# A planned attention kernel: its layout table found anew, five transfer charges raised, and a guard on the units that VectorE takes

## The chip, the cores and the metric

The kernel runs on one core of one Trainium2 chip. The core has TensorE (PE, matrix products), VectorE (DVE), ScalarE (ACT), GpSimd (POOL) and SyncE (SP, which here only issues transfers). The metric is the device time of one execution in microseconds (us); lower is better.

## The reference

Two attention layers read the same x of 2048 tokens by 640, each with 32 heads of 20. A is full softmax attention. B lets each token see 8 earlier ones at a distance of 2. A gate per token mixes the two.

```python
g = sigmoid((x * gate_w).sum(-1, keepdims=True))
# A: o = softmax(q @ k.T * 20**-0.5) @ v over all 2048 keys, 32 heads
# B: keys at pos - 2*w, w = 0..7, masked below 0; softmax over these 8
# both: q, k, v = x @ wqkv, and o (heads side by side) @ wo
return g * A(x, A_wqkv, A_wo) + (1 - g) * B(x, B_wqkv, B_wo)
```

Nearly all the work is A: 32 heads of 2048 by 2048 scores, each through an exponential.

## The kernel before

**Groups and units.** A is cut into 32 groups: four stretches of 512 queries (qc) by eight sets of four heads (q). A group has 64 units; a unit is 128 keys by 512 queries of one head. TensorE makes a unit's scores in PSUM (line 1600), its exponential is taken, and the product with the values (with a column of ones for the denominators) is summed in one PSUM bank, `obank` (line 1669).

**Two ways to an exponential.** ScalarE takes two or three units in one instruction, which is called a tile here (line 1624; 1024 or 1536 elements a partition). The other way is VectorE's: a unit that rides in the third bank of a tile's scores becomes a 16-bit integer whose bits are read as bf16 (line 1614, `uD`), and three shifted copies of it (line 863, `eD`) are averaged with it by values that GpSimd has weighted (line 855, `vS`). Four such units, with the same keys, make a quad. A quad is opened in `wanted()` for the present group or the next one, from the last keys of the group backwards; the products take the quads strictly in the order in which they were opened (`pv_slot`).

**What else runs.** Between the tiles come the projections of A (lines 660 to 792), layer B in eight units of 256 tokens (products of q with shifted k on VectorE at line 935, their sums on TensorE at 945, maxima at 970 to 978, exponentials at 983, products with v at 1032, their sums at 1042, the division at 1065), the end of each group (transpose of `obank` at 824, division on GpSimd at 830 and 836, transpose back at 838, transfer to `oTd` at 841), and the products with both wo (`gen_fold`; for the last 512 tokens `gen_prefold` and `gen_prefold2`, whose results the tail completes at line 1148). Where TensorE would stand idle too long the planner puts products that nobody reads (`filler`, line 1690).

**The planner.** No order is written by hand. While the program is built, `task()` keeps a clock for each engine with a charged duration for each instruction, and a loop over tiles picks what comes next. Its choices hang on 18 numbers (how long TensorE may be kept from the next scores, when a third unit or a ride is taken, priorities of the side work, the load below which fillers are put in, and so on). `PLAN` gives them by tile number: an entry holds from its tile on until the next entry. The clock and the choices exist only at build time. The chip runs five fixed lists of instructions, one an engine, each in order, which wait for each other by semaphores alone.

**Lists of transfers.** Five places issue several small transfers in a row from SP, which count as one task: rows of q to `qT` (730), bounds to `qT` (770), a group's output to `oTd` (841), B's reciprocals to `rB` (1018) and their spreading to all partitions (1020). Each is charged 2.0 us and some time per transfer until all have landed.

**The end.** `gen_wl` loads the last rows of A's wo into a buffer (`woA_l`) that is also an output buffer: GpSimd clears it (1114) once the output has left, and SP loads it (1115). `gen_prefold` makes the products of the last 512 tokens in three pieces (columns 0 to 511 of token blocks 0 and 1, then columns 512 to 639 of all four blocks), and `gen_prefold2` blocks 2 and 3. The third piece and `gen_prefold2` need B's last unit.

Of the kernel before, what the change touches and what calls it, by code (L numbers as in the profile page):

```python
# [50 lines left out]
    0: ((0.29, 0.69), 0.16, 1.0, 5.5, 0.94, -1.37, 0.17, 9.99, 5.5, 6.98, 0.6, 0.62, 5.69, 5.04, 0.0, 0.62, 2, -1.5),  # L51
    5: ((0.29, 0.69), 0.01, 1.0, 6.6, 1.12, -1.6, 0.17, 11.8, 2.0, 7.54, 0.6, 0.62, 4.85, 4.42, 0.0, 0.65, 2, -3),
    15: ((0.32, 0.64), 0.16, 1.0, 2.5, 0.94, -1.41, -0.97, 11.8, 7.0, 8.62, 0.62, 0.47, 4.4, 4.29, 0.0, 0.54, 2, -3),
    20: ((0.29, 0.69), 0.16, 1.0, 2.5, 0.94, -1.41, -0.97, 11.8, 7.0, 8.62, 0.62, 0.62, 5.69, 5.04, 0.0, 0.54, 2, -3),
    30: ((0.3, 0.63), 0.25, 1.0, 2.5, 1.39, -1.06, -0.43, 7.4, 7.0, 8.84, 0.7, 0.51, 4.4, 4.81, -0.2, 0.69, 1, -3),
    35: ((0.32, 0.68), 0.31, 2.5, 5.5, 0.76, -1.58, -0.5, 11.8, 7.0, 6.64, 0.35, 0.39, 4.4, 4.35, 0.0, 0.66, 2, -3),
    40: ((0.34, 0.69), 0.01, 1.0, 5.5, 0.94, -1.37, 0.17, 9.99, 7.0, 7.54, 0.6, 0.62, 5.69, 5.04, 0.0, 0.65, 2, -3),
    45: ((0.26, 0.66), 0.39, 1.0, 2.5, 0.49, -1.34, -0.97, 7.4, 7.0, 8.25, 0.52, 0.47, 4.4, 4.0, 0.0, 0.71, 3, 0.0),
    50: ((0.26, 0.75), 0.39, 1.0, 2.5, 0.49, -1.34, -0.97, 7.4, 7.0, 8.25, 0.52, 0.47, 4.4, 4.0, 0.0, 0.71, 3, 0.0),
    60: ((0.26, 0.75), 0.39, 1.0, 2.5, 0.49, -1.34, -0.97, 6.5, 7.0, 8.25, 0.43, 0.47, 4.4, 4.0, 0.0, 0.71, 3, 0),  # L60
    70: ((0.26, 0.75), 0.39, 1.0, 2.5, 0.81, -1.34, -0.97, 6.5, 7.0, 8.25, 0.43, 0.47, 4.4, 4.0, 0.0, 0.71, 0, 0),
    75: ((0.25, 0.75), 0.39, 1.0, 2.5, 0.81, -1.34, -0.97, 6.61, 7.0, 8.25, 0.43, 0.47, 4.4, 4.0, 0.0, 0.71, 0, 0),
    85: ((0.32, 0.64), 0.16, 1.0, 6.6, 0.94, -1.41, -0.97, 11.8, 7.0, 8.62, 0.62, 0.47, 4.4, 4.29, 0.0, 0.54, 3, -3),
    90: ((0.3, 0.63), 0.07, 5.5, 6.3, 0.94, -1.06, 0.05, 7.4, 2.0, 8.96, 0.66, 0.67, 4.79, 5.42, -0.14, 0.53, 1, -1.5),
    100: ((0.3, 0.63), 0.07, 2.5, 6.3, 0.94, -1.06, 0.05, 11.8, 2.0, 6.64, 0.44, 0.67, 3.3, 3.84, -0.14, 0.66, 1, -3),
    105: ((0.3, 0.63), 0.07, 5.5, 6.3, 0.94, -1.06, 0.05, 9.51, 2.0, 8.96, 0.64, 0.67, 3.3, 5.42, -0.14, 0.53, 1, -1.5),
    110: ((0.32, 0.64), 0.16, 5.5, 2.5, 0.94, -1.06, 0.05, 11.8, 2.0, 8.96, 0.62, 0.67, 3.3, 5.42, -0.14, 0.53, 2, -3),
    115: ((0.3, 0.66), 0.25, 2.5, 2.5, 0.73, -1.17, 0.49, 7.4, 2.0, 5.3, 0.63, 0.52, 5.64, 3.24, 0.0, 0.61, 1, 0),
    120: ((0.29, 0.69), 0.16, 1.0, 1.0, 0.94, -1.37, 0.17, 9.99, 7.0, 7.54, 0.6, 0.62, 5.69, 5.04, 0.0, 0.65, 2, -3),
    125: ((0.29, 0.69), 0.16, 1.0, 1.0, 0.94, -1.37, 0.17, 9.99, 7.0, 7.54, 0.6, 0.53, 5.69, 5.04, 0.0, 0.65, 2, 0),  # L70
    135: ((0.29, 0.6), 0.16, 1.0, 1.0, 0.94, -1.37, 0.17, 9.99, 7.0, 7.54, 0.6, 0.47, 5.69, 5.04, 0.0, 0.65, 2, 0),
    140: ((0.29, 0.6), 0.16, 1.0, 1.0, 0.94, -1.37, 0.17, 9.99, 7.0, 7.54, 0.6, 0.47, 5.69, 5.2, 0.0, 0.6, 2, 0),
    145: ((0.29, 0.6), 0.16, 1.0, 1.0, 0.94, -1.37, 0.17, 9.99, 2.0, 8.47, 0.6, 0.47, 5.69, 5.2, 0.0, 0.6, 2, 0),
    150: ((0.23, 0.7), 0.25, 2.5, 2.5, 0.83, -1.37, 0.49, 7.4, 5.5, 6.11, 0.45, 0.67, 7.13, 5.42, 0.0, 0.61, 1, 0),
    155: ((0.23, 0.7), 0.16, 1.0, 2.5, 0.94, -1.37, 0.49, 7.4, 5.5, 7.54, 0.45, 0.67, 5.69, 5.04, 0.0, 0.54, 1, -3),
    180: ((0.23, 0.7), 0.16, 1.0, 2.5, 0.94, -1.37, 0.49, 7.4, 5.5, 7.54, 0.45, 0.67, 5.69, 5.04, 0.0, 0.54, 1, 1),
    185: ((0.23, 0.7), 0.16, 5.5, 2.5, 0.94, -1.37, 0.49, 7.4, 5.5, 7.54, 0.45, 0.67, 5.69, 5.04, 0.0, 0.54, 1, -3),
    190: ((0.23, 0.7), 0.28, 5.5, 1.0, 0.94, -1.6, -0.5, 7.4, 5.5, 7.54, 0.52, 0.67, 4.64, 5.04, 0.0, 0.54, 1, -1.5),
    200: ((0.32, 0.64), 0.35, 5.5, 1.0, 0.94, -1.6, -0.5, 11.8, 7.0, 7.54, 0.52, 0.67, 4.4, 5.04, 0.0, 0.54, 1, -1.5),
    210: ((0.33, 0.64), 0.35, 5.5, 1.0, 1.02, -1.6, -0.5, 11.8, 7.0, 7.54, 0.52, 0.67, 4.4, 5.04, 0.0, 0.54, 1, -1.5),  # L80
    215: ((0.31, 0.76), 0.28, 2.5, 1.0, 0.72, -1.6, -0.65, 9.86, 7.0, 7.05, 0.52, 0.55, 5.68, 3.17, 0.0, 0.64, 2, -6),
    220: ((0.34, 0.68), 0.38, 2.5, 1.0, 0.94, -1.06, 0.05, 7.4, 7.0, 10.69, 0.6, 0.55, 3.3, 5.42, 0.0, 0.61, 1, -1.5),
    225: ((0.34, 0.68), 0.38, 2.5, 1.0, 0.82, -1.06, -0.35, 9.79, 7.0, 10.69, 0.61, 0.44, 4.4, 5.42, 0.0, 0.61, 1, 1),
    245: ((0.34, 0.68), 0.38, 2.5, 1.0, 0.82, -1.06, -0.35, 6.21, 7.0, 10.69, 0.61, 0.44, 4.4, 5.42, 0.0, 0.53, 1, 1),
    250: ((0.44, 0.72), 0.28, 2.5, 1.0, 1.21, -1.6, -0.5, 9.86, 7.0, 6.01, 0.45, 0.54, 6.04, 3.66, 0.0, 0.87, 0, -6),
    255: ((0.34, 0.68), 0.38, 2.5, 1.0, 0.94, -1.06, 0.05, 7.4, 7.0, 10.69, 0.6, 0.55, 3.3, 5.42, 0.0, 0.61, 1, -1.5),
    260: ((0.3, 0.63), 0.39, 1.0, 2.5, 0.94, -1.26, -0.43, 7.8, 7.0, 6.29, 0.7, 0.73, 5.56, 4.87, -0.08, 0.67, 2, -3),
    265: ((0.3, 0.63), 0.16, 1.0, 1.0, 0.94, -1.46, -0.29, 6.5, 5.5, 7.16, 0.43, 0.75, 6.57, 3.11, -0.2, 0.43, 1, 0),
    270: ((0.3, 0.63), 0.25, 1.0, 1.0, 0.94, -1.29, -0.29, 6.5, 5.5, 7.16, 0.43, 0.75, 6.57, 3.83, -0.2, 0.43, 1, 0),
    275: ((0.3, 0.63), 0.25, 1.0, 1.0, 0.94, -1.29, -0.29, 6.5, 5.5, 7.16, 0.43, 0.75, 6.57, 3.83, -0.2, 0.56, 1, 0),  # L90
    280: ((0.3, 0.63), 0.25, 2.5, 1.0, 0.94, -1.29, 0.49, 6.5, 5.5, 7.16, 0.43, 0.75, 5.56, 3.83, 0.0, 0.61, 1, 0),
    285: ((0.3, 0.63), 0.38, 2.5, 1.0, 0.94, -1.29, 0.49, 6.5, 5.5, 7.16, 0.43, 0.63, 5.56, 4.3, 0.0, 0.61, 1, 0),
    290: ((0.23, 0.63), 0.38, 2.5, 1.0, 0.94, -1.29, 0.49, 6.5, 5.5, 7.16, 0.43, 0.63, 5.56, 4.3, 0.0, 0.61, 0, 0),
    295: ((0.23, 0.63), 0.1, 2.5, 1.0, 0.94, -1.29, 0.49, 6.5, 5.5, 7.16, 0.43, 0.63, 5.56, 4.3, 0.0, 0.61, 0, 0),
    300: ((0.23, 0.63), 0.1, 2.5, 1.0, 0.94, -1.29, 0.49, 6.5, 5.5, 7.16, 0.43, 0.63, 5.56, 4.3, 0.0, 0.77, 0, 0),
    305: ((0.23, 0.66), 0.25, 2.5, 2.5, 0.94, -1.05, 0.49, 7.4, 2.0, 5.3, 0.43, 0.43, 5.56, 3.83, -0.1, 0.61, 1, 0),
# [283 lines left out]
def _build(ctx, nc, A_x, A_wqkv, A_wo, B_wqkv, B_wo, gate_w, out):  # L380
# [252 lines left out]
    done = {}  # L633
# [840 lines left out]
    def wanted(js):  # L1474
# [8 lines left out]
        if not dopen:  # L1483
# [4 lines left out]
            for g in range(cur["g"], min(NG, cur["g"] + 2)):  # L1488
                lo, hi = ahead[g]
                t_end += (4 * hi - lo - 4) * UNIT  # L1490
                if done.get(("q", g)) and t_end >= now + DTIME:
                    break
# [370 lines left out]
```

## Time and profile before

| | |
|---|---|
| median of 3 runs | 810.18 us (809.9 to 811.21) |
| the profiled execution's own time | 810.18 us |
| its span (first to last instruction) | 808.3 us |
| ACT busy | 779.0 us |
| PE busy | 749.0 us |
| DVE busy | 721.9 us |
| POOL busy | 129.3 us |
| share of the 16 DMA engines' span taken by the main queue | 17.0% |
| tiles of 1024 and of 1536 | 449 and 258 |
| rides (`uD`) and shifted copies (`eD`) | 376 and 282 |
| filler products on TensorE | 480 (120 sets of four) |
| granted TensorE clock, mean | 0.996 |

Busy time adds up an engine's records. Records of ScalarE and VectorE reach into those that follow, so a busy share near 100% still hides short waits; the distance between two starts shows what one instruction really takes. TensorE's four 32-column products run side by side, so four records cost about what one does. The column "idle before" names what ended an engine's last wait.

### The profile page before, as it was taken

Reading aid. Unit: us, or ns where it says so; the run is one execution under the profiler, and the core shown is the slowest. Engines: PE = TensorE matmul, PEld = TensorE weight load, DVE = VectorE, ACT = ScalarE, POOL = GpSimd, SP = SyncE. Lnnn points to the kernel's source line nnn. Section 1 sums busy time; section 2 is a strip of 40 time slices with the busy share of each in tenths; the row PEclk is TensorE's granted clock in tenths of the full one; section 3 lists DMA queues with packets and bytes.
Section 4 is the critical chain, followed back from the end, with each engine's and each line's share of the span. In section 5 each row is a group of like instructions: output and inputs, shape, how many; then the busy total and the mean of one; then the engine's idle time right before and its main releaser. Section 6 shows DMA issues by size and latency. Waiting matters only on the chain.

```text
span 808.3 us, 28593 instructions
## 1 busy us (share of the span) xinstructions
PE 749.0 (93%) x12063; PEld 285.9 (35%) x12065; DVE 721.9 (89%) x1236; ACT 779.0 (96%) x739; POOL 129.3 (16%) x193
## 2 busy tenths in 40 slices
PE   8999999999899898999999898999899899999987
PEld 5432222333233332333334323432334343234323
DVE  7587996589999999999999999899999999998865
ACT  4999999999999999999999999999999999999994
POOL 6011011011121110212112111121111212111010
PEclk9999999999999999999999999999999999999999
DMA  9112112300013131110013101313010310300221
GB/s 310 45 28 44 43 29 47 76 13 20 5 39 73 34 69 34 21 25 6 22 37 70 24 18 30 77 22 68 7 39 26 71 23 18 74 7 23 51 55 37
DMA packets 61458, 35.50 MB, mean 44 GB/s; under 512 B 27220, under 2 KB 60132, under 8 KB 61332
## 3 DMA queue, kind: packets, MB, share of 16 engines
q1 hardware_dynamic: 61044, 33.36, 17.0%
q8 instruction: 96, 1.57, 0.8%
q10 hardware_dynamic: 288, 0.33, 0.1%
q14 instruction: 30, 0.25, 0.1%
HBM read 12.00 MB, written 2.62 MB: 18 GB/s over the span
## 4 chain that ended last, share of the span: by engine, by line
PE 34%; DVE 32%; ACT 20%; issue 11%; SPq 1%; DMA 1%; POOL 0%; DVEq 0%; ACTq 0%; POOLq 0%
ACT ebuf L1624 20%; DVE uD L1614 12%; PE score L1600 10%; DVE eD L863 9%; PE side L623 9%; PE obank L1669 9%; PE score L623 3%; DVE kvw L935 3%; DVE kvw L1032 2%; DVE qkvB L909 2%; SPq L917 1%; PE obank L1690 1%; PE score L1315 1%; PE obank L523 1%; PE side L1042 1%
## 5 line engine op out<-in xcount | busy, mean ns | idle before, releaser
L1624 ACT ACTIVATE ebuf<-score 128x1024 bf16<-128x1024 f32 (+1 forms) x707 | 767.2, 1233 | 8.6 <-PE score L1600 7.4
L1600 PE MATMUL score<-qT,kT 32*128 32x512 bf16 x2048 | 278.5, 385 | 32.5 <-ACT ebuf L1624 19.5
L1614 DVE TENSOR_SCALAR uD<-score 128x512 int16<-128x512 f32 x376 | 247.3, 677 | 12.3 <-PE score L1600 11.9
L863 DVE TENSOR_SCALAR eD<-uD 128x2048 int16<-128x2048 int16 x282 | 200.2, 731 | 1.7 <-PE obank L1669 0.6
L1669 PE MATMUL obank<-ebuf,vA 128*21 128x512 bf16 x1672 | 155.7, 387 | 4.8 <-DVE oTt L824 1.3
L1600 PEld LDWEIGHTS score<-qT,kT 32*128 32x128 bf16 x2048 | 69.6, 91 | 255.7 <-ACT ebuf L1624 177.7
L855 POOL TENSOR_TENSOR vS<-vA,vw 128x252 bf16<-128x252 bf16 x94 | 70.0, 748 | 317.5 <-PE obank L1669 261.5
L1669 PE MATMUL obank<-eD,vS 128*21 128x512 bf16 x1128 | 99.4, 382 | 0.0
L623 PE MATMUL side<-xT,wBs 128*32 128x256 bf16 x2400 | 96.5, 282 | 2.3 <-DVE qkvB L909 1.5
L623 PEld LDWEIGHTS side<-xT,wBs 128*32 128x32 bf16 x2400 | 68.1, 142 | 33.1 <-issue 16.3
L1669 PEld LDWEIGHTS obank<-ebuf,vA 128*21 128x21 bf16 x1672 | 36.8, 89 | 88.0 <-issue 60.4
L830 POOL TENSOR_TENSOR rcp<-rcp,gA 128x16 f32<-128x16 f32 x31 | 8.3, 268 | 292.2 <-DVE rcp L828 292.2
L935 DVE TENSOR_TENSOR kvw<-qkvB 128x2048 bf16<-128x2048 bf16 x40 | 48.6, 1233 | 0.0
L1032 DVE TENSOR_TENSOR kvw<-kvw,eB 128x2048 bf16<-128x2048 bf16 x40 | 47.9, 1213 | 0.5 <-DMA kvw<-qkvB 0.5
L909 DVE CAST qkvB<-side 128x512 bf16<-128x512 f32 (+1 forms) x72 | 41.6, 587 | 5.1 <-PE side L623 4.9
L1669 PE MATMUL obank<-uD,vA 128*21 128x512 bf16 x376 | 36.8, 382 | 0.1
L1669 PEld LDWEIGHTS obank<-eD,vS 128*21 128x21 bf16 x1128 | 27.9, 92 | 17.1 <-issue 1.0
L836 POOL TENSOR_TENSOR oN<-oTt,rcp 128x512 bf16<-128x512 f32 x31 | 32.7, 1053 | 2.4
L824 DVE STREAM_TRANSPOSE oTt<-obank 128x512 f32<-128x512 f32 x32 | 22.6, 706 | 4.3 <-PE obank L1669 4.3
L623 PE MATMUL side<-woBp,oB 128*32 128x512 bf16 (+1 forms) x500 | 25.4, 304 | 0.9 <-DVE outsb L1193 0.5
L623 PE MATMUL side<-woA_d,oTd 128*32 128x512 bf16 (+1 forms) x496 | 25.5, 303 | 0.0
L623 PE MATMUL side<-xT,kvw 128*32 128x512 bf16 x310 | 24.3, 382 | 0.9 <-DVE qkvB L660 0.3
(180 smaller groups left out, 517.4 us busy)
## 6 DMA issues: line engine op xcount, KB each, us to landing
kvw<-qkvB SPq DMA_DIRECT2D x128, 80.6 KB
WqP<-in_A_wqkv_dram SPq DMA_DIRECT2D x16, 160.0 KB
wBs<-in_B_wqkv_dram SPq DMA_DIRECT2D x1, 2400.0 KB
oTd<-oN SPq DMA_DIRECT2D x108, 20.0 KB
qT<-dst SPq DMA_DIRECT2D x104, 20.0 KB
out_dram<-outsb SPq DMA_DIRECT2D x12, 160.0 KB
kvw<-in_A_wqkv_dram SPq DMA_DIRECT2D x2, 800.0 KB
oTd<-in_A_x_dram SPq DMA_DIRECT2D x2, 640.0 KB
```

The source lines that it names most:

```text
L623: ins = e.matmul(o[j:k, :], l(j) if callable(l) else l[:, j:k], r, start=(first and i == 0), stop=(last and i == n - 1), skip_group_check= ...
L824: T("dve", 0.625, lambda e: e.transpose(oTt[:, :], obank[:, :]), reads=["obank"], writes=["oTt"])
L836: T(en, c2, lambda e: e.tensor_tensor(oo, ii, ib, ALU.mult), reads=["rcp", "oTt"], writes=["oN0"])
L855: T("pool", 0.607, lambda e: e.tensor_tensor(vS[:, d % 2, :, :], _ap(vA, (kb * NQ + q) * 4 * DV, [[0, K - 1], [1, 4 * DV]]), _ap(vw, 0, [[ ...
L863: T("dve", 0.065 + 0.1334 * n, lambda e, k=k, sl=sl: e.tensor_scalar(eD[:, sl % NS, 0:512 * n].bitcast(I16), uD[d % 2][:, 0:512 * n].bitca ...
L909: t = TB(dvc(n * TOK), lambda e, o=o, i=i: e.tensor_copy(o, i), reads=[("side", b)], writes=[key])
L935: TB(dvc(CH, 2), lambda e: e.tensor_tensor(o, i0, i1, ALU.mult), reads=["qB", "kB"], writes=[("prod", i)] + (["WkA", "WvA", ("WkP", 0)] if ...
L1032: TB(dvc(CH, 2), lambda e: e.tensor_tensor(o, i0, i1, ALU.mult), reads=["eB"] + [("vR", w4) for w4 in range(4)], writes=[("prod", i)], por ...
L1600: ins = e.matmul(o, kT[32 * j:32 * j + 32, q, kb * P:(kb + 1) * P], qT[g % NQT][32 * j:32 * j + 32, :], start=True, stop=True)
L1614: t = T("dve", 0.598, lambda e: e.tensor_scalar(uD[d % 2][:, 512 * i:512 * (i + 1)].bitcast(I16), side[x], UOFF, 0.0, op0=ALU.add, op1=ALU ...
L1624: exps[s] = T("act", actc(512 * n), lambda e: e.activation(ebuf[s % NE][:, 0:512 * n], score[s % 2][:, 0:512 * n], ACTF.Exp, scale=LN2 / S ...
L1669: ins = e.matmul(obank[32 * j:32 * j + DV, :], v, src, start=(kb == 0), stop=(last and k >= len(lst) - 4), skip_group_check=True)
```

## The change

There are three edits.

1. Every entry of `PLAN` is replaced. The old table has 102 entries, the new one 110; no entry is the same.
2. The charge per transfer in five lists is raised: 0.5 to 0.74 us (730), 0.63 (770), 0.72 (841), 0.62 (1018), 0.6 (1020). This moves the planner's clock only; the transfers themselves stay as they are.
3. In `wanted()`, a quad can be opened for a group only if the last quad was not opened for a later one.

In the changed kernel all lines behind the table stand 8 lower than before; this document keeps the old numbers up to the result.

```diff
 PLAN = {
-    0: ((0.29, 0.69), 0.16, 1.0, 5.5, 0.94, -1.37, 0.17, 9.99, 5.5, 6.98, 0.6, 0.62, 5.69, 5.04, 0.0, 0.62, 2, -1.5),
...
+    705: ((0.32, 0.68), 0.31, 6.3, 5.5, 0.94, -1.49, -0.5, 11.8, 7.0, 7.19, 0.52, 0.43, 6.31, 4.87, 0.0, 0.9, 1, 0),
 }
...
-                T("sp", 2.0 + 0.5 * len(pc), lambda e, i=i, pc=pc, qc=qc: [e.dma_start(
+                T("sp", 2.0 + 0.74 * len(pc), lambda e, i=i, pc=pc, qc=qc: [e.dma_start(
...
-                T("sp", 2.0 + 0.5 * 4 * len(runs), lambda e, runs=runs, qc=qc: [e.dma_start(
+                T("sp", 2.0 + 0.63 * 4 * len(runs), lambda e, runs=runs, qc=qc: [e.dma_start(
...
-            T("sp", 2.0 + 0.5 * len(pc), lambda e: [e.dma_start(
+            T("sp", 2.0 + 0.72 * len(pc), lambda e: [e.dma_start(
...
-        T("sp", 2.0 + 0.5 * 4, lambda e: [e.dma_start(rB[0:32, j * TQ:(j + 1) * TQ], rQ[32 * j:32 * j + 32, :]) for j in range(4)],
+        T("sp", 2.0 + 0.62 * 4, lambda e: [e.dma_start(rB[0:32, j * TQ:(j + 1) * TQ], rQ[32 * j:32 * j + 32, :]) for j in range(4)],
...
-        spread = lambda: T("sp", 2.0 + 0.5 * 3, lambda e: [e.dma_start(rB[32 * i:32 * i + 32, :], rB[0:32, :]) for i in range(1, 4)],
+        spread = lambda: T("sp", 2.0 + 0.6 * 3, lambda e: [e.dma_start(rB[32 * i:32 * i + 32, :], rB[0:32, :]) for i in range(1, 4)],
...
-                if done.get(("q", g)) and t_end >= now + DTIME:
+                if done.get(("q", g)) and t_end >= now + DTIME and (not dquads or dquads[-1][0] <= g):
```

What the planner makes of it, counted in the lists of instructions:

| | before | changed |
|---|---|---|
| tiles of 1024 / 1536 / 512 elements | 449 / 258 / 0 | 463 / 249 / 1 |
| rides `uD` | 376 | 374 |
| shifted copies `eD` of 2048 / 1024 elements | 282 / 0 | 279 / 3 |
| filler products (sets of four) | 120 | 91 |
| products of all other kinds, less the two kinds of A's values | the same | the same |
| transfers | the same | the same |
| `gen_prefold`'s third piece, 160 products of 128 columns | after the last tile | between the last five tiles |
| `gen_prefold2`, 80 products of 512 columns | after the last tile | 4 before the last tile's scores, 12 before the last product with the values, 64 after it |
| clearing of `woA_l` on GpSimd (1114) | two weighted-value instructions (855) behind it | the last instruction there |
| B's last unit: first sum of q by k (945), first sum of v (1042) | tile 684 and 697 of 707 | tile 670 and 697 of 713 |

Tiles are numbered from 0. Nearly every row of every list stands elsewhere than before. With the old table, the guard changes no instruction, and the charges change only the order of the last fourteen tiles.

## The prediction

> **What bounds the kernel now.** I read the page's busy times first, then the groups by form for ScalarE, its timeline, the waits, and the chain and timelines of the last 40 us.
>
> ```profile
> PE 749.0 (93%) x12063; PEld 285.9 (35%) x12065; DVE 721.9 (89%) x1236; ACT 779.0 (96%) x739; POOL 129.3 (16%) x193
> L1624 ACT ACTIVATE ebuf<-score 128x1024 bf16<-128x1024 f32 x449 | 435.9, 1080 | 4.6 <-PE score L1600 3.6
> L1624 ACT ACTIVATE ebuf<-score 128x1536 bf16<-128x1536 f32 x258 | 365.5, 1500 | 4.0 <-PE score L1600 3.8
> ...
> 19.47 1.45 ACT L1624 ACTIVATE ebuf<-score 128x1536 bf16<-128x1536 f32 x1 [2.00 <-PE score L1600]
> 333.99 2.95 ACT L1624 ACTIVATE ebuf<-score 128x1536 bf16<-128x1536 f32 x2
> 335.32 2.96 ACT L1624 ACTIVATE ebuf<-score 128x1536 bf16<-128x1536 f32 x2
> 576.22 0.71 ACT L983 ACTIVATE eB<-side 128x512 bf16<-128x512 f32 x1
> 576.70 2.07 ACT L1624 ACTIVATE ebuf<-score 128x1024 bf16<-128x1024 f32 x2
> 578.51 0.38 ACT L1010 ACTIVATE tB<-side 128x64 f32<-128x64 f32 x1
> ```
>
> ScalarE looks full, but its records overlap: two tiles of 1024 take 1.81 us from start to start (576.70 to 578.51), 0.904 each, where the mean record is 1.080; a tile of 1536 takes 1.331 (333.99 to 335.32), not 1.500. The tiles run from 19.47 to 795.72 (last start 794.39 and 1.33), 776.25 us. Of these 449 x 0.904 = 405.9 and 258 x 1.331 = 343.4 are tiles, about 5 the other instructions (0.48 for each of eight `eB`, 0.1 for the small ones). **The other 22 us are waits**, 67 of them over 0.1 us, most too short for the idle columns, which show only 8.6. So the time is: 19.5 before the first tile, 749.3 of tiles, 5 of other, 22 of waits, 12.6 behind the last tile. The profiled execution took 810.18 us, 1.9 more than its span of 808.3, and is the median of the runs, so the sum is made against 810.18.
>
> The end:
>
> ```profile
> 788.81 0.69 DVE L1065 SCALAR_TENSOR_TENSOR oB<-side,rB 128x512 bf16<-128x512 f32 x1 [1.35 <-DMA rB<-rB]
> ...
> 795.99 0.61 PE obank L1669 x8
> 796.60 2.23 PE score L623 x160
> 798.83 2.16 PE side L623 x40
> 800.99 2.16 PE score L623 x40
> 803.15 0.22 PE score L1148 x16
> ...
> 798.70 0.45 DVE L838 STREAM_TRANSPOSE oN<-oN 128x256 f32<-128x256 f32 x1
> ```
>
> Behind the last product with the values, 6.55 us of `gen_prefold` and `gen_prefold2` (the three L623 rows) stand on TensorE before L1148. VectorE has the last group's output ready at 799.15, and L1148 waits 4 us more for TensorE. This is the only place where the end is TensorE's.
>
> And 20 us earlier:
>
> ```profile
> 772.41 0.36 POOL L1114 MEMSET outsb<- 128x320 f32 x1 [23.55 <-DMA out_dram<-outsb]
> 772.74 0.61 POOL L855 TENSOR_TENSOR vS<-vA,vw 128x252 bf16<-128x252 bf16 x1
> 773.40 0.40 PE L1669 MATMUL obank<-ebuf,vA 128*21 128x512 bf16 x4 [1.31 <-POOL vS L855]
> 770.19 4.14 ACT L1624 ACTIVATE ebuf<-score 128x1536 bf16<-128x1536 f32 x3 [0.44 <-PE score L1600]
> 774.60 2.79 ACT L1624 ACTIVATE ebuf<-score 128x1536 bf16<-128x1536 f32 x2 [0.27 <-PE score L1600]
> 779.09 1.02 ACT L1624 ACTIVATE ebuf<-score 128x1024 bf16<-128x1024 f32 x1 [0.29 <-PE score L1600]
> ...
> 776.00:778.00 2.00, 2.00 (x22) 0.42 (x18) 1.06 (x2) 2.00 (x4) 0.00 (x0) 0.52 0.07 16
> ```
>
> GpSimd waits for an output transfer before it may clear the buffer (1114); the weighted values (855) stand behind that, TensorE waits for them, and then runs at half clock (0.52 is the granted clock in 776 to 778; its matmuls come 0.43 apart instead of 0.22). ScalarE loses 0.42 (770.19 and 3 x 1.331 end at 774.18, the next starts at 774.60), then 0.43 before 779.09 and 0.17 twice: 1.2 us.
>
> **The change part by part.**
>
> *More and smaller tiles.* 463 x 0.904 + 249 x 1.331 + one of 512 at 0.48 (as `eB`) = 750.4 against 749.3: **+1.1 us**, on ScalarE, which sets the end. Two rides fewer and three half-sized copies take 2 x 0.60 + 3 x 0.27 = 2.0 us from VectorE. I cost this at nothing: ScalarE hides it, and VectorE only counts where it delays scores. The 29 filler sets that go (29 x 0.216 = 6.3 us of TensorE) were put where it would stand idle: nothing either, unless the clock falls.
>
> *The end.* The third piece of `gen_prefold` (2.23) now stands between the last five tiles, and 16 of the 80 products of `gen_prefold2` before the last product with the values (four sets, 0.86); one set of that product (0.22) goes too. Behind the last tile there remain 0.27 of hand-over, 0.22 and 16 sets x 0.216 = 3.45 before L1148, against 795.72 to 803.0 now: 3.9 instead of 7.2, **-3.3 us**. VectorE's chain from the last product to the transposed output took 3.2 us (795.99 to 799.15), so TensorE stays the last by half a microsecond; from below the gain is bounded by that chain, from above by 2.3 if the tiles pay 1 us for the pieces between them.
>
> *GpSimd.* The clearing is now its last instruction, nothing stands behind it, so this wait of TensorE goes: **-1.2 us** for ScalarE; 0 if another wait lands at the same place, no more than 1.9 with the 0.67 us wait at 768.6 before it. The load behind it has over ten tiles, some 10 us, for a transfer out and one in, which took about 5.
>
> *The charges.* The rows bear them out: seven transfers of 730 issue in 5.22 us (0.75 each), five of 841 in 3.87 (0.77), four of 1018 in 2.48 (0.62), three of 1020 in 1.77 (0.59). But in the trace one instruction alone waited for such a list, VectorE for `rB` at 788.81, 1.35 us, so what truer charges can save by themselves is at most that. In SP's list the spreading (1020) now stands behind five transfers of 841 and two outputs: 3.87 + 1.07 + 3.04 (from 785.77 to 788.81) = 8.0 us after the transpose (838), where VectorE has about 4 us of work before it needs `rB`. So this wait grows to 2.4 to 4 us. I cost it at nothing: no ride stands behind it in VectorE's order, and TensorE comes to the results five tiles later. Without that cover it costs up to 2.6.
>
> *The guard.* Alone it changes nothing; with the new table it keeps a quad for an earlier group from standing behind one for a later group, where the products could never take it. No time.
>
> *All other tiles.* Nearly every gap between two tiles' scores holds other work on TensorE now, and no row of before shows these gaps. I bound them by counting. For each gap I took TensorE's work in the changed order (0.216 us for a set of four 512-column products, 0.056 for 128 columns, 0.21 for two changes between kinds), 1.1 us for the scores and hand-overs, and subtracted ScalarE's time for the two tiles that cover it; and the same over two gaps. Before, 173 of 704 gaps come out at zero or more, nine of them at 0.4 or more, and 0.05, 0.13 and 0.15 us of wait follow on the average in the classes 0 to 0.2, 0.2 to 0.4 and above. In the new order 208 of 710 do, 15 at 0.4 or more. With the averages of all classes the waits go from 20.8 to 22.2: **+1.4 us**. Lower end -2 (before's worst places, like the half clock at 317 us below, do not return), upper end +5 (rival 1). I take the count, since it comes from 704 gaps.
>
> Sum: 810.18 + 1.1 - 3.3 - 1.2 + 1.4 = **808.2 us**, 0.25% less.
>
> **The clock.** The trace has two stretches of 3.4 us at half clock, from 317.1 and from 774.5:
>
> ```profile
> 316.30 0.39 PE L1600 MATMUL score<-qT,kT 32*128 32x512 bf16 x3 [0.82 <-DVE uD L1614]
> 318.00:320.00 2.00, 2.00 (x22) 0.44 (x18) 1.92 (x4) 1.60 (x3) 0.61 (x1) 0.50 0.00 1
> ```
>
> Both follow thin stretches: over four tiles TensorE's work is 56% of ScalarE's time at tile 269 and 40% at 686. The new order has 53% at 231 and 59% at 400 as its lowest, so I expect one such stretch, not two. The Trainium skill (TensorE: Matmul & The Clock Gate, section "HAM oscillation") gives as the abstract rule no idle gaps over about 3.4 us; here waits of 0.82 and 1.31 us went before, so the trace does not agree. By that rule the GpSimd wait did not lower the clock, and the time would be rival 3's, 809.0.
>
> **The rivals.**
> 1. *TensorE is late in the filled gaps* (the other side). Place: the 208 gaps, above all tiles 400 to 500 with eight of the highest class against four. If each of the 35 more costs the 0.13 of the next class and the six more of the highest the 0.5 of the worst waits seen, that is 4.6 + 3.0 instead of 1.4: 814.4. The forecast has 22.2 us of waits between the tiles (22 - 1.2 + 1.4); from 24.2 on this rival decides the sign, and above 25.8 the time is over 0.2% longer. For it: mean and number of full gaps rise. Against it: before, such gaps mostly cost nothing (135 of them 0.05).
> 2. *The end is not shorter*: the wait for `rB` reaches the last tiles (2.6), or the products between them cost what they save. 810 to 811. For it: the longer list on SP. Against it: five tiles of cover.
> 3. *The halving at 774 does not hang on GpSimd's wait*: then only the wait's own 0.42 goes, 0.8 of the 1.2 stays, 809.0. For it: tile 691 also has four filler sets in front of the next scores, which cost time at any clock. Against it: TensorE stood still for 1.31 us right before. The skill's rule above speaks for this one.
> 4. *VectorE becomes the bound* in tiles 227 to 327, where its work is 1.04 of ScalarE's tiles; but it was 1.03 in 411 to 511, without more waits there (1.2 us in 40 tiles): below 1 us, inside the range.
>
> **How the numbers follow.** About 0.2% (1.6 us) is what a measurement of this kernel can tell from no change. The forecast (end shorter, waits between 18.9 and 22.6 us) 0.46, below 808.6; its own range is 805 to 808.5. Within 0.2%, 0.28: rival 2 0.10, rival 3 0.06, the forecast with waits up to 25.8 0.12. Rival 1 beyond that: 0.24, mostly 812 to 814; rival 4 beyond its bound 0.02; together 0.26. The range leaves out one in ten on either side: 804.8 to 813.0.
>
> **What would show it.** Right: L1148 starts about 3.9 us behind the last tile's end; 455 to 465 tiles of 1024; no L855 behind L1114; waits of the tiles summing to 19 to 23 us; `rB` as VectorE's longest transfer wait. Wrong: waits above 24.2 us; three or more stretches at half clock; a wait of TensorE for oB or `rB` results in the last 20 us.

## The result, and the profile after

The changed kernel takes 812.8 us (median of 16 runs, 809.69 to 815.77) against 809.88 us before (16 runs beside them, 807.85 to 811.36): a ratio of 1.0038, 95% interval 1.0025 to 1.0051. It is slower by 0.4%, where 0.25% faster was forecast. Run again on another occasion it gave 1.0032 (1.0017 to 1.0046). From here on the line numbers are those of the changed kernel, 8 higher than before, and those of before only where a kernel with the old table is spoken of.

The profiled execution took 812.49 us, 2.3 more than that of before. Worked out from starts, as in the prediction:

| us | before | after | |
|---|---|---|---|
| up to the first tile | 19.47 | 19.43 | 0 |
| the tiles themselves | 749.3 | 750.4 | +1.1 |
| ScalarE's other instructions between tiles | 5.0 | 5.0 | 0 |
| waits between tiles | 21.85 | 25.88 | **+4.0** |
| last tile's end to L1148 (now L1156) | 7.26 | 3.84 | -3.4 |
| from there to the end of the span | 5.30 | 6.10 | +0.8 |
| around the span | 1.9 | 1.7 | -0.2 |

The busy times and groups by form of the changed kernel, which answer to the first lines shown of before:

```profile
PE 746.2 (92%) x11943; PEld 282.5 (35%) x11943; DVE 711.6 (88%) x1234; ACT 780.4 (96%) x745; POOL 133.0 (16%) x193
L1632 ACT ACTIVATE ebuf<-score 128x1024 bf16<-128x1024 f32 x463 | 450.5, 1088 | 6.4 <-PE score L1608 5.1
L1632 ACT ACTIVATE ebuf<-score 128x1536 bf16<-128x1536 f32 x249 | 354.0, 1520 | 5.9 <-PE score L1608 5.6
L1622 DVE TENSOR_SCALAR uD<-score 128x512 int16<-128x512 f32 x374 | 246.9, 678 | 25.0 <-PE score L1608 24.5
```

The tiles are as forecast. Less work on VectorE (711.6 us for 721.9) did not help: what it has lost in work it now spends waiting, 24.5 us for TensorE's scores in front of `uD` where it was 11.9. ScalarE's idle time in front of tiles is 12.3 us instead of 8.6, and these columns hold only part of its waits.

The end, in the timelines of TensorE, VectorE and GpSimd after:

```profile
799.91 0.38 PE L1608 MATMUL score<-qT,kT 32*128 32x512 bf16 x1
800.22 0.83 PE L631 MATMUL side<-woBp,oB 128*32 128x512 bf16 x12
801.03 0.40 PE L1677 MATMUL obank<-ebuf,vA 128*21 128x512 bf16 x4
...
804.49 0.39 PE L631 MATMUL score<-WqP,oTd 128*32 128x512 bf16 x4
804.70 0.40 PE L1156 MATMUL score<-outsb,oN 128*32 128x128 bf16 x16
...
803.51 0.45 DVE L846 STREAM_TRANSPOSE oN<-oN 128x256 f32<-128x256 f32 x1
...
783.37 0.36 POOL L1122 MEMSET outsb<- 128x320 f32 x1 [6.84 <-DMA out_dram<-outsb]
```

L1156 starts 3.84 us behind the last tile (800.86), and the transposed output stands ready at 803.96: TensorE is still the last, by 0.7 us. GpSimd's wait for the output transfer is still there, but nothing stands behind it.

Some 15 us earlier, VectorE, TensorE and ScalarE:

```profile
787.11 0.69 DVE L1073 SCALAR_TENSOR_TENSOR oB<-side,rB 128x512 bf16<-128x512 f32 x1 [5.77 <-DMA rB<-rB]
...
787.86 0.61 PE L631 MATMUL side<-woBp,oB 128*32 128x512 bf16 x8 [0.49 <-DVE oB L1073]
788.40 0.39 PE L1608 MATMUL score<-qT,kT 32*128 32x512 bf16 x3
...
788.84 3.71 ACT L1632 ACTIVATE ebuf<-score 128x1536 bf16<-128x1536 f32 x3 [0.68 <-PE score L1608]
792.96 8.01 ACT L1632 ACTIVATE ebuf<-score 128x1536 bf16<-128x1536 f32 x7 [0.41 <-PE score L1608]
```

VectorE waits 5.77 us for `rB`, TensorE then 0.49 for VectorE's result, and the scores queued behind it come 0.80 us late (0.54 at 792.96). And one of the worst places in the middle, a gap with five sets of products and three of `gen_fold`, in the timelines of TensorE and ScalarE:

```profile
559.30 0.40 PE L631 MATMUL side<-woBp,oB 128*32 128x512 bf16 x4
559.52 0.60 PE L631 MATMUL side<-woA_d,oTd 128*32 128x512 bf16 x8
559.95 0.61 PE L1677 MATMUL obank<-ebuf,vA 128*21 128x512 bf16 x8
560.38 0.39 PE L1677 MATMUL obank<-uD,vA 128*21 128x512 bf16 x4
560.60 0.61 PE L1677 MATMUL obank<-eD,vS 128*21 128x512 bf16 x8
561.14 0.39 PE L1608 MATMUL score<-qT,kT 32*128 32x512 bf16 x3
...
561.58 1.02 ACT L1632 ACTIVATE ebuf<-score 128x1024 bf16<-128x1024 f32 x1 [0.99 <-PE score L1608]
```

TensorE never stands still there: eight sets of work stand in front of the scores at 561.14, and ScalarE waits 1.19 us.

Each wait between tiles can be put down to what TensorE did in the 2.6 us ahead of it. **Behind TensorE's own work** stand 10.1 us before and 12.0 after; where **TensorE itself waited for VectorE**, 6.8 and 10.0; in **stretches at half clock**, 2.1 and 1.35. The rest, 2.9 and 2.5 us, is not sorted. So most of the growth, 3.2 of the 4.0 us, first shows where TensorE waited for VectorE, and only 1.9 behind TensorE's own work.

### The profile page after: what moved, and what is told of

The parts are those of the page before. It is cut to its first block, busy times and chain, and to the rows that moved or that the text cites. A ratio compares the mean times of both kernels' runs of the same rounds, so it can differ in the third digit from the quotient of the medians.

```text
span 810.8 us, 28367 instructions
## 1 busy us (share of the span) xinstructions
PE 746.2 (92%) x11943; PEld 282.5 (35%) x11943; DVE 711.6 (88%) x1234; ACT 780.4 (96%) x745; POOL 133.0 (16%) x193
## 4 chain that ended last, share of the span: by engine, by line
PE 33%; DVE 27%; ACT 22%; issue 12%; SPq 4%; DMA 1%; POOL 0%; DVEq 0%; ACTq 0%; POOLq 0%
ACT ebuf L1632 22%; PE score L1608 10%; DVE uD L1622 9%; PE obank L1677 9%; PE side L631 8%; DVE eD L871 7%; PE score L631 4%; SPq L925 3%; DVE kvw L943 2%; DVE qkvB L917 2%; DVE kvw L1040 1%; DVE oTt L832 1%; SPq L778 1%; PE score L1323 1%; PE obank L531 1%
## 5 line engine op out<-in xcount | busy, mean ns | idle before, releaser
L1632 ACT ACTIVATE ebuf<-score 128x1024 bf16<-128x1024 f32 (+1 forms) x713 | 769.0, 1238 | 12.3 <-PE score L1608 10.7
L1608 PE MATMUL score<-qT,kT 32*128 32x512 bf16 x2048 | 282.2, 385 | 39.5 <-ACT ebuf L1632 27.9
L1622 DVE TENSOR_SCALAR uD<-score 128x512 int16<-128x512 f32 x374 | 246.9, 678 | 25.0 <-PE score L1608 24.5
L871 DVE TENSOR_SCALAR eD<-uD 128x2048 int16<-128x2048 int16 x282 | 191.1, 703 | 2.7 <-PE obank L1677 1.8
L863 POOL TENSOR_TENSOR vS<-vA,vw 128x252 bf16<-128x252 bf16 x94 | 73.1, 782 | 314.3 <-PE obank L1677 261.3
L1040 DVE TENSOR_TENSOR kvw<-kvw,eB 128x2048 bf16<-128x2048 bf16 x40 | 48.9, 1241 | 1.4 <-DMA kvw<-qkvB 1.4
L631 PE MATMUL side<-woBp,oB 128*32 128x512 bf16 (+1 forms) x440 | 23.6, 309 | 1.3 <-DVE oB L1073 0.5
L631 PE MATMUL side<-xT,WqP 128*32 128x512 bf16 x320 | 24.2, 382 | 0.6 <-DVE qkvB L917 0.5
L631 PE MATMUL side<-woA_d,oTd 128*32 128x512 bf16 (+1 forms) x432 | 22.9, 307 | 0.0
```

The source lines that it names most:

```text
L631: ins = e.matmul(o[j:k, :], l(j) if callable(l) else l[:, j:k], r, start=(first and i == 0), stop=(last and i == n - 1), skip_group_check= ...
L863: T("pool", 0.607, lambda e: e.tensor_tensor(vS[:, d % 2, :, :], _ap(vA, (kb * NQ + q) * 4 * DV, [[0, K - 1], [1, 4 * DV]]), _ap(vw, 0, [[ ...
L871: T("dve", 0.065 + 0.1334 * n, lambda e, k=k, sl=sl: e.tensor_scalar(eD[:, sl % NS, 0:512 * n].bitcast(I16), uD[d % 2][:, 0:512 * n].bitca ...
L1040: TB(dvc(CH, 2), lambda e: e.tensor_tensor(o, i0, i1, ALU.mult), reads=["eB"] + [("vR", w4) for w4 in range(4)], writes=[("prod", i)], por ...
L1608: ins = e.matmul(o, kT[32 * j:32 * j + 32, q, kb * P:(kb + 1) * P], qT[g % NQT][32 * j:32 * j + 32, :], start=True, stop=True)
L1622: t = T("dve", 0.598, lambda e: e.tensor_scalar(uD[d % 2][:, 512 * i:512 * (i + 1)].bitcast(I16), side[x], UOFF, 0.0, op0=ALU.add, op1=ALU ...
```

## The experiments

The theory at this point is rival 1: the new order fills more gaps and leaves less slack. Against it stand three narrower ones: the waits are a few misplaced instructions; VectorE's results come too late; the half clock.

### The wait for `rB` taken away

```diff
+            if u == 2 * QCN - 1:
+                i1 = _ap(tB, 0, [[0, n], [0, TOK]])
...
+            if u == 2 * QCN - 1:
+                t.deps = [d for d in t.deps if d.dom != "dma"]
```

> The changed kernel in the same order, but the division of the last unit (line 1073) reads a buffer that has long been there in place of `rB` (so its last 256 tokens of oB come out with other factors), and does not wait for the transfer. In the changed kernel VectorE waited 5.77 us here, and ScalarE lost 0.80 us before 788.84 and 0.54 before 792.96. If the wait for `rB` is what these two waits come from, both fall below 0.2 us, the waits between tiles go from 25.9 to about 24.6, and the time from 812.8 to 811.5 (ratio to before 1.002). If the pieces of gen_prefold between the last tiles are the cause, whoever waits for `rB`, the two waits stay and the time stays at 812.8 (1.0036).

Measured: 812.07 us, ratio 1.0033 (1.0019 to 1.0047). ScalarE's timeline of this kernel:

```profile
783.59 8.43 ACT L1636 ACTIVATE ebuf<-score 128x1536 bf16<-128x1536 f32 x7
792.43 2.79 ACT L1636 ACTIVATE ebuf<-score 128x1536 bf16<-128x1536 f32 x2 [0.41 <-PE score L1612]
```

Seven tiles now run on without a break where the 0.80 us wait was; the 0.54 us wait is still there. So the transfer costs 0.8 us of ScalarE's time, not 1.3, and it is a small part of the loss. The sum of the waits does not show even this: it is 26.2 us in this profile, which has two stretches at half clock where the changed kernel's has one, and the time lies between the two forecasts.

### The clearing moved, alone

```diff
+    pool.append(pool.pop(at(pool, 1114)))
+    load = sp.pop(at(sp, 1115))
+    sp.insert(at(sp, 841) + 1, load)
```

> The kernel before, with one part of the new order alone: GpSimd clears the buffer (1114) as its last instruction, and the load behind it (1115) stands behind the last transfers of 841 on SP. If the prediction's step is right, L855 no longer waits for the output transfer, TensorE's wait of 1.31 us and the half clock from 774.5 go, and the time falls by 1.2 us, to 808.7 (0.9985). If the half clock does not hang on that wait (rival 3), only 0.4 us go, 809.5. If the load of the rows now lands too late, L1148 waits for it and the time rises.

Measured: 808.69 against 809.18 us in the runs beside it, ratio 1.0 (0.9985 to 1.0014). TensorE no longer waits for L855. The windows of this kernel (the column behind POOL's is the granted clock):

```profile
770.00:772.00 2.00, 1.03 (x15) 0.20 (x7) 1.86 (x5) 2.00 (x3) 1.67 (x3) 1.00 0.32 108
772.00:774.00 2.00, 1.82 (x19) 0.54 (x19) 2.00 (x5) 2.00 (x3) 0.00 (x0) 0.63 0.03 7
774.00:776.00 2.00, 2.00 (x18) 0.57 (x18) 0.21 (x1) 2.00 (x3) 0.00 (x0) 0.51 0.06 14
```

The half clock is still there, from 772.5. Rival 3 is right: it did not hang on GpSimd's wait. The time, 0.5 us less, is not to be told from no change. ScalarE's waits at this place say why: the one of 0.4 us in front of 774.60 is gone, and the next one, 0.43 us before, is now 0.88.

### The charges alone, with the old table

```diff
-        spread = lambda: T("sp", 2.0 + 0.5 * 3, ...
+        spread = lambda: T("sp", 2.0 + 0.6 * 3, ...
```

(and the four other charges; no change to the table; the guard is in it too, which with the old table changes no instruction under these charges either)

> The old table with the new charges of the lists of transfers: the order changes in the last 14 tiles alone. If truer charges are worth what the one transfer wait of before shows, the time falls by up to 1.35 us (808.5 to 809.9, ratio 0.998 to 1). If the planner, now expecting `rB` later, puts work behind it that TensorE must then do after the last tile, the part from the last tile to the end grows beyond 12.6 us and the time rises by as much, 1 to 3 us (1.001 to 1.004).

Measured: 814.68 us, ratio 1.0065 (1.0051 to 1.0079), 5.5 us more than before in the same runs, above both forecasts. The timelines of TensorE and VectorE at the end of this kernel, and its windows (columns as above):

```profile
795.25 0.39 PE L1042 MATMUL side<-kvw,Rep 128*32 128x256 bf16 x8
798.29 0.72 PE L623 MATMUL score<-woBp,oB 128*32 128x128 bf16 x20 [2.65 <-DVE oB L1065]
...
797.85 0.39 DVE L1065 SCALAR_TENSOR_TENSOR oB<-side,rB 128x256 bf16<-128x256 f32 x1
...
796.00:800.00 4.00, 1.71 (x68) 1.71 (x72) 2.10 (x6) 0.00 (x0) 0.00 (x0) 0.55 0.00 0
800.00:804.00 4.00, 4.00 (x128) 3.21 (x124) 0.69 (x1) 0.00 (x0) 0.00 (x0) 0.60 0.02 4
```

With truer charges the planner expects `rB` a little later, and puts VectorE's last division (1065) behind the transposing and scaling of the last group. TensorE waits 2.65 us for it, falls to half clock, and does the products that were left for the end at that pace.

### The same, with the one instruction back in its place

```diff
+    t = dve.pop(ids.index(4723))
+    dve.insert(ids.index(4716), t)
```

(4723 is the last 1065, 4716 the transpose 824.)

> The old table with the new charges took 814.7 us, 5.5 more than before in the same runs: VectorE's last division (1065) had moved behind the transposing and scaling of the last group (824 to 838), TensorE waited 2.65 us for it at 798.29, and two stretches at half clock followed. Here that one instruction stands ahead of 824 again, all else in the order of the charges. If its place is the price of the charges, TensorE's wait of 2.65 falls below 0.7, the half clock goes or shrinks to one stretch, and the time falls to 809.5 to 811 (ratio 1.0005 to 1.002). If the charges cost through the order of the last 14 tiles, the time stays above 813.

Measured: 810.35 us, ratio 1.0015 (1.0003 to 1.0027). 4.3 us come back by moving one instruction five places: its place is most of the price of the charges. Some 0.7 us are left against before.

### The new table with the old charges

> The new table with the charges of before, and the guard. If a table serves for any charges, as good an order comes out as with the new charges: 811 to 815 us. If it fits only the charges with which it was found, the planner's choices at one place change all behind it: 820 us or more, with more rides left out (719 tiles in place of 712) and more waits.

Measured: 848.53 us in a single execution, 38.8 more than before. The waits between tiles are 43 us, 21 more; and the tiles themselves take 767.0 us, 17.7 more, because 274 of them are of 1536. So far off, one execution is enough: under the old charges the new table gives a far worse order.

### Five instructions moved

```diff
+    ahead("dve", 473, 470)
+    ahead("dve", 3876, 3872)
+    ahead("sp", 4600, 4598)
+    ahead("pe", 3307, 3319)
+    ahead("pe", 3308, 3319)
```

> The changed kernel with five instructions moved by hand: the transposing of the output (832) one place forward in VectorE's order at 77 and 656 us; two sets of fold products of the gap at 559 us behind the next two tiles' scores; the spreading of `rB` (1028) ahead of the two output transfers. The waits there were 0.75, 0.62, 1.19 and, at the end, 0.80 and 0.54. If the 4.0 us that the waits grew by belong to single places where the new order puts an instruction too late, these become about 0.5, 0.1, 0.5 and together 0.7 at the end: 2.1 us less, the waits 23.8, the time 810.7 (1.001). If they belong to a general backlog of TensorE in filled gaps, the waits turn up again within the next few tiles, their sum stays within 0.7 of 25.9, and the time within 0.7 of 812.8.

Measured: 812.74 us, ratio 1.0042 (1.0026 to 1.0057). The waits went from 0.75 to 0.60 (tile 54), 0.62 to under 0.4 (587), 1.19 to 0.96 (496) and 0.80 to under 0.4 at the end; but a wait of 0.94 us for L1040 stood newly at 783.7, and the sum was 26.8 us, with one more stretch at half clock than in the changed kernel's profile. Nothing was gained. The fall at tile 587 is not even owed to the move: in two other executions of the new order, in which nothing was moved there, that wait is 0.10 and 0.15 us.

### Less work for VectorE, in both orders

```diff
-                eD[:, sl % NS, 0:512 * n].bitcast(I16), ...
+                eD[...].rearrange("p (i c) -> p i c", c=512)[:, :, 0:256].bitcast(I16), ...
-                src = eD[:, sl, 512 * i:512 * (i + 1)] if k else ...
+                src = _ap(eD, sl * 2048 + 512 * i, [[0, 2], [1, 256]]) if k else ...
```

> The kernel before in its own order, but line 863 writes `eD` for the first 256 of each 512 tokens only, and the products read these twice (so the second halves are computed with the first halves' values). VectorE does some 282 x 0.3 = 85 us less, TensorE and ScalarE the same. It is half of a pair with the changed kernel. Of the 21.9 us of waits between tiles, the 6.8 in which TensorE itself waits for VectorE should fall to 2 to 4: a time of 806 to 808.

> The other half of the pair: the changed kernel with the same cut in VectorE's work. If its longer waits come from VectorE's results standing too late in the new order (10.0 us of them against 6.8), the relief takes away more here than in the kernel before: the waits fall from 25.9 to within 1 us of those of the pair's other half, the time falls by 5 us or more from 812.8, and what is left of the difference is tiles +1.1 and end -2.6: the changed kernel is then 0.5 to 1.5 us the faster of the pair. If TensorE's own backlog in filled gaps is the cause (rival 1), both fall alike and the changed kernel stays 2 to 4 us the slower of the pair.

Measured: 802.21 us (0.9911, 0.9894 to 0.9927) in the old order and 807.83 us (0.9977, 0.9964 to 0.9989) in the new. The changed kernel is 5.6 us the slower of the pair. From the views of waits (us in total, times, longest), the old order first:

```profile
DVE uD L1615 <- PE score L1601: 35.2, 85, 1.4
...
ACT ebuf L1625 <- PE score L1601: 4.1, 6, 2.0
```

```profile
DVE uD L1623 <- PE score L1609: 53.8, 107, 1.6
...
ACT ebuf L1633 <- PE score L1609: 9.5, 15, 2.1
```

With VectorE's load cut, both engines wait for TensorE's scores, and in the new order more: VectorE 53.8 us against 35.2, ScalarE 9.5 against 4.1. The waits between tiles are 13.1 us, none of them at half clock, against 21.9, of which 3.3 at half clock; 5.4 us of difference remain without these, against 4.8 in the full kernels (19.7 and 24.5 without theirs). So cutting VectorE's load does not bring the orders together: the forecast of 0.5 to 1.5 us the faster fails, and the 5.6 us lie above the 2 to 4 of rival 1 too. What separates the orders is not VectorE's load alone. The waits where TensorE waited for VectorE fall to about 1 and 3 us here, and most of the difference now stands behind TensorE's own work (9.5 and 13.2).

### Less work for VectorE and TensorE, in both orders

```diff
-                ins = e.matmul(obank[32 * j:32 * j + DV, :], v, src,
+                ins = e.matmul(obank[32 * j:32 * j + DV, 0:src.shape[-1]], v, src,
```

(and `src` 256 columns wide for `eD`)

> The kernel before in its own order, with VectorE's work cut as in the pair with half-width shifts (802.2 us there), and now the products with `eD` are 256 columns wide too (the output bank gets them for the first half of the tokens only). TensorE does 282 sets x 0.108 = 30 us less, spread over the tiles. In the pair with half-width shifts TensorE's own work stood for 9.5 us of the waits here. If these are a backlog, they fall to 5 to 8; the stretches at half clock may become more, since TensorE fills less of the time.

> The changed kernel with the same two cuts. With VectorE's alone it took 807.8 us, and of its 21.9 us of waits 13.2 followed on TensorE's own work, 3.7 more than in the kernel before. If that difference is a backlog of TensorE (rival 1), it shrinks here with TensorE's load, to 2 or less: the waits behind TensorE's work come to 6 to 9 us. If it lies in the order in which ScalarE and TensorE hand tiles to each other, whatever the load, it stays at 3 or more.

Measured: 801.53 us (0.9893, 0.9865 to 0.992) and 806.69 us (0.9958, 0.9939 to 0.9976). The waits behind TensorE's own work fell from 9.5 to 8.1 in the old order and from 13.2 to 10.4 in the new: 2.3 us apart instead of 3.7, between the two forecasts. All waits away from the half clock stand 11.9 against 14.3, 2.4 apart instead of 5.4. So the difference does shrink with TensorE's load. In the medians it does not show (5.2 us apart), because the thinner work of TensorE came with more stretches at half clock in the new order (7.4 us of waits in the profile, 2.0 in the old). Executions of like mean clock do show it: at 0.995 to 0.996 the old order takes 801.08 and 801.33 us and the new one 803.07; at 0.991 to 0.993, 801.73 against 803.73 and 804.54. That is 2 to 3 us apart, where the pair with VectorE's load alone cut is about 5 apart. These are few executions.

### The crowded gaps split

Sorted by what stands in the gap, the waits of the changed kernel are larger in one kind above all: four sets of products between two tiles of 1024, ten of them and one like it at 0.52 us on the average; before there are six, at 0.23. One of the eleven, in front of tile 213, waits 1.35 us because a stretch at half clock falls on it. Here are ScalarE and the window (column of the granted clock as above) of the changed kernel, then ScalarE in another execution of it (the unchanged kernel run again, below), without a stretch there:

```profile
251.67 1.45 ACT L1632 ACTIVATE ebuf<-score 128x1536 bf16<-128x1536 f32 x1 [1.24 <-PE score L1608]
250.00:252.00 2.00, 2.00 (x19) 0.37 (x11) 1.70 (x4) 0.76 (x2) 0.00 (x0) 0.50 0.15 33
...
251.94 17.55 ACT L1632 ACTIVATE ebuf<-score 128x1536 bf16<-128x1536 f32 x16 [0.17 <-PE score L1608]
```

There the wait is 0.28 us, worked out from starts, and the average over the eleven 0.42.

```diff
...
+                pe[pe.index(t)] = _Task(t.idx, "pe", "cmp", issue(lst[:12], False), t.deps)
+                t.fn = issue(lst[12:], last)
+                pe.insert(pe.index(scores[s]) + 1, t)
```

> The changed kernel, where in eleven gaps (in front of tiles 37, 165, 191, 213, 229, 301, 393, 419, 431, 496, 539) what pv issues as four or five sets of products between two tiles' scores is issued in two parts: three sets where they were, the rest behind the next scores. In the trace of the changed kernel these eleven waits are 0.39, 0.51, 0.32, 1.35, 0.59, 0.32, 0.61, 0.33, 0.61, 1.19 and 0.34, 6.6 us in all, or 5.5 in an execution in which the half clock does not fall on tile 213; the kernel before has six such gaps, 1.4 us. If these gaps are what rival 1's class averages missed, each falls to 0.2 or less, the waits between tiles fall by 2.5 to 3.5 us and the time to 809.3 to 810.3 (ratio 0.9995 to 1.0007). If TensorE's backlog is general, the moved sets make the next gap late instead, and the time stays within 0.8 of 812.8.

Measured: 813.39 us, ratio 1.0047 (1.0031 to 1.0063). Against another execution of the new order (that without the wait for `rB`), the eleven waits fell from 5.5 to 2.7 us, but the four tiles behind each gave back 1.1 of it, and the time did not fall.

> The kernel before with the clearing last on GpSimd, and the same splitting at its own six gaps of four sets that cost 0.26 us or more (tiles 44, 59, 325, 425, 655, 693; together 2.1 us). With each at 0.1 or less this takes 1.2 to 1.7 us from 808.7: 807.0 to 807.5 (ratio 0.9965 to 0.998), a kernel faster than both. If splitting only shifts the waits, it stays at 808.7.

Measured: 808.17 us, ratio 0.9987 (0.9975 to 1.0): not to be told from before.

### The half clock

```diff
...
+    for idx, n in ((1872, 3), (4601, 1), (4602, 4)):
+        p = [t.idx for t in pe].index(idx) + 1
+        pe[p:p] = [_Task(idx, "pe", "cmp", still, []) for _ in range(n)]
```

> The kernel before with the clearing last on GpSimd (808.7 us, and still two stretches at half clock, from 315.1 and 772.5) and eight more filler sets on TensorE, each adding zeros to the output bank: three in front of the scores at 314.7, five around those at 770.8 and 772.2, where TensorE stands still for 0.81, 0.19 and 0.95 us. In every run so far a stretch at half clock is one of a row of intervals of 3.413 us and stands behind one in which full-speed products fill less than some 0.49 of the time. If that is what lowers the clock, both stretches go, 2.1 us of waits with them less some 0.3 for the sets, and the time falls to about 807.0 (ratio 0.997 to 0.998). If the clock hangs on something else, the stretches stay and the time is 808.7 or a little more.

Measured: 808.61 us, ratio 0.9988 (0.9973 to 1.0003). Both stretches went; the windows of this kernel at the second place:

```profile
770.00:772.00 2.00, 2.00 (x34) 0.53 (x22) 1.90 (x6) 2.00 (x3) 1.27 (x3) 1.00 0.16 52
772.00:774.00 2.00, 2.00 (x33) 0.75 (x34) 1.80 (x4) 2.00 (x2) 0.00 (x0) 1.00 0.04 10
774.00:776.00 2.00, 2.00 (x58) 0.82 (x46) 0.00 (x0) 2.00 (x4) 0.00 (x0) 1.00 0.08 20
```

But in this execution another stretch began at 792.4 and slowed the end. Of the twelve executions seven list a mean clock of 0.999 or more, against two of twelve with the clearing alone, so the fillers do keep the clock up more often; what this saves in time is within the noise.

> The kernel before with the clearing last, the eight filler sets in front of the two thin places, which took both stretches of half clock away there, and six more filler sets between the last tiles (789 to 792 us), where a stretch now stood in front of the end (from 792.4, behind an interval filled to 0.34) and made the part behind the last tile 14.2 us instead of 12.5. If the filling of the interval decides, no stretch is left between 20 and 800 us in nearly every execution, and the time is 806.5 to 807.5 (ratio 0.996 to 0.998), below both kernels. If not, it stays at 808.6.

Measured: 811.17 us, ratio 1.001 (0.9993 to 1.0026), against the forecast. The stretch at the end was gone in the profile, but two others in a row stood at 521 us, behind a wait of 1.59 us for a transfer to VectorE, and TensorE stood still for 0.94 us inside `gen_prefold2` for no reason that the profile shows.

### All reliefs together, beside the changed kernel

> The changed kernel itself, unchanged, as the measure for the next run on the same chip: 812 to 813.5 us (ratio 1.0025 to 1.005), 25 to 26.5 us of waits between tiles, of these 5 to 6 in the eleven gaps, 0.8 and 0.54 at the end.

> The changed kernel with all that was tried singly: the eleven gaps split, two fold sets moved out of the gap at tile 496, the transposing one place forward at tiles 54 and 587, and no wait for `rB` in the last unit (whose last 256 tokens of oB come out with other factors). If the 4 us of longer waits lie in these places, what was measured singly adds up: 1.6 net from the gaps, 0.3 at tile 496, 0.6 at tile 587, 0.9 at the end, 3.4 us less waits, 22 to 23 in all at an equal number of half-clock stretches, and 809 to 810 us (0.999 to 1.0005). If each relief is handed on as the next wait, the waits stay above 24 and the time above 811.3.

Measured: 812.08 us (1.0032, 1.0017 to 1.0046) and 811.71 us (1.0031, 1.0019 to 1.0043). The waits were 25.5 us, with no stretch at half clock between the tiles, and 26.9, of which 2.2 at half clock: leaving the half clock aside some 0.8 us less, where 3.4 was expected. How a relief is handed on is seen at tile 496, in the timelines of ScalarE and TensorE of the kernel with all reliefs:

```profile
562.55 2.10 ACT L1636 ACTIVATE ebuf<-score 128x1024 bf16<-128x1024 f32 x2 [0.33 <-PE score L1612]
565.15 2.85 ACT L1636 ACTIVATE ebuf<-score 128x1024 bf16<-128x1024 f32 x3 [0.50 <-PE score L1612]
...
563.51 1.26 PE L631 MATMUL side<-woA_d,oTd 128*32 128x512 bf16 x20
564.71 0.39 PE L1612 MATMUL score<-qT,kT 32*128 32x512 bf16 x3
```

The wait of 1.19 us has become one of 0.54, and the two fold sets that were moved make a new one of 0.61 two tiles later. They found no slack near by. Of the versions that do the whole work, none is faster than the kernel before by more than its measurement can tell.

## Why the prediction was wrong, point by point

**More and smaller tiles, +1.1: right.** 750.4 us, 463 tiles of 1024.

Between the forecast of 808.2 us and the profiled execution's 812.49 lie 4.3 us: 3.7 are waits between tiles that were forecast too low and 0.8 the end behind L1148; the other terms together are 0.2 below the forecast.

**The end, -3.3: right up to L1148, and 0.8 given back behind it.** L1156 starts 3.84 us behind the last tile (3.9 forecast). But from the issue of the last output transfers (805.01 before, 806.73 after) to the end of the span it takes 4.07 us instead of 3.27, in every such trace (4.09 and 4.13 in two more of the new order, 3.29 in another of the old). I had taken what lies behind L1148 as unchanged.

**GpSimd, -1.2: wrong in the reason, and the sum is not shown.** In the new order the wait and the half clock are gone from there, but so is the old order of all that stood around them. Moved alone, the clearing takes the wait for GpSimd away and leaves the half clock, and ScalarE loses the same 1.2 us there as before. Rival 3 was right on the mechanism, at a chance of 0.06.

**The charges, "at most 1.35": the bound had one side only.** I asked what truer charges could save and not what they could cost. With the old table they cost 5.5 us, nearly all of it through the place of one instruction. Under the same charges the table found anew is 2.7 us the faster. That the new table had to pay for the charges first is a reading of these two numbers; no run shows it, and in the new order that one instruction stands elsewhere.

**The `rB` wait, costed at nothing: wrong.** It grew to 5.77 us (2.4 to 4 forecast), and cost 0.8 us between tiles. The cover that was counted on is there, but not for so long: in the kernel with the split gaps the same wait was 4.16 us, and ScalarE lost 0.13 by it. A wait of TensorE for an oB result in the last 20 us was named as a sign of this; the one that came (0.49 us) stands 23 us before the end.

**All other tiles, +1.4: the step that failed.** The waits came to 25.88 us, not 22.2. The count of gaps was right and two of the three classes of full gaps cost what they had cost: 170 gaps of 0 to 0.2 at 0.049 us (0.05 assumed), 15 of the highest at 0.135 (0.15). The 23 of 0.2 to 0.4 cost 0.28 each and not 0.13, which is 3.3 of the 3.7 us; 1.1 of these 3.3 is the half clock that fell on tile 213, so the gaps themselves account for some 2.2. Nearly all of it lies in the eleven gaps with four sets, of which before showed six. An average over 29 gaps of mixed content did not stand for 11 of one kind. Nor would the six have been enough: at their 0.23 the eleven come to 2.5 us, and without the half clock they took 4.6. Gaps were counted one by one, where their neighbours decide whether lost time is caught up.

This is rival 1 (814.4 at its full price, its mark for over 0.2% at 25.8 us of waits). The runs bear it out in part: the difference outlives the cut in VectorE's load, shrinks when TensorE's is cut too, and is handed on from place to place. Against it stands that in the full kernels most of the growth shows where TensorE waits for VectorE, which itself waits longer for TensorE's scores (24.5 us for 11.9): the two cannot be told apart there. Splitting the fullest gaps did not shorten the time. So a backlog of TensorE is the likelier cause, not a shown one. Which of the new table's numbers brings it about stays open.

**The clock: one stretch in the profile, as forecast, but not where it was looked for.** It stands at tile 213, not at the thin places at 231 and 400, and another execution of the same order has none, so the match is luck. Over all executions it is no cause of the loss. Spans by mean granted clock, of all executions of the two kernels in which it is listed:

| mean clock | before: executions, mean span us | after |
|---|---|---|
| 0.999 and more | 6, 806.1 | 12, 809.8 |
| 0.997 to 0.998 | 43, 806.8 | 5, 811.5 |
| 0.995 to 0.996 | 43, 807.9 | 6, 811.0 |
| below | 18, 809.5 | 5, 813.0 |

At equal clock the changed kernel is 3 to 5 us longer; it has more executions without half clock, which hides a part of that.

## What to carry to other kernels

A planner's charges and the numbers tuned under them are one thing: a charge that is nearer to the trace can move one late instruction to a worse place and cost more than its error ever did, so cost both sides of it, and look at what the order does at the end. Waits that are handed on cannot be priced by an average per gap: where a kind of gap becomes more frequent, price it by the few of exactly that kind, take even that for a low figure (here it gave about half), and ask whether the next gaps have room. A wait read in a single trace may be that execution's own: read the same place in a second execution before moving anything for it. A wait that disappears with a change is not thereby explained; undo it alone, and look whether the next wait has grown by as much.

## What the runs showed of the hardware

**The half clock comes in fixed intervals.** Between the first tiles and the end of the kernel every stretch lasted 3.413 us or twice that, and within an execution their starts differ by whole multiples: 774.489 - 317.103 = 457.386 = 134 x 3.4133 before, 492.279 - 273.826 = 218.453 = 64 x 3.4133 without the wait for `rB`. The Trainium skill (TensorE: Matmul & The Clock Gate, section "What's actually happening") describes a free-running window of 3413 ns; the traces agree. It also has the clock fall after an idle window; here it fell behind intervals that full-speed products (0.216 us for a set of 512 columns) filled to about 0.25 to 0.48, far from idle, and filling two of them with eight sets of zeros kept it up. Some intervals filled to 0.38 to 0.44 had no stretch behind them, so this share is not the whole of the rule. The intervals do not start with the kernel: the same thin place of the old order has its stretch at 317.103 us before and at 315.146 with the clearing moved, which leaves 3.08 and 1.12 us over whole intervals. So one order can have different numbers of stretches: the changed kernel shows one in one trace and none in another. A stretch of 3.413 us at half clock takes 0.002 from the mean clock, and by the table above that costs about 1 us.

**The end behind the last output transfers took 0.8 us longer in the new order.** Counted from the issue at 805.01 before and at 806.73 after, the last packets of the output end after 2.15 and 2.56 us, SyncE's wait for them after 2.51 and 3.04, and the span after 3.27 and 4.07. In the last microseconds of the new order the profile counts two packets on the instruction queue, and one in the old; the additional one runs from 1.73 to 2.04 us, while the output is still on its way. Whether that is the cause was not tried.
